# Late expert jobs of a fused retention, GLU and expert kernel: new order on the engine queues, the shared term kept in PSUM, unit 0 stores on ScalarE's queue

## The chip, the cores and the metric

The kernel runs on one core of a Trainium2 chip. The metric is the device time of one execution in microseconds (us). Five engines work side by side, each through a queue of its own in program order: PE (TensorE, matmuls into PSUM), DVE (VectorE), ACT (ScalarE), POOL (GpSimd) and SP (SyncE, which here only issues DMAs). Semaphores order them where one needs another's data or buffer.

## The reference

Retention over 4 x 8 heads of 576 positions gives 2304 tokens of 512 features; a gated unit follows; then the experts, where the late jobs of this case lie:

```python
P = np.exp(logits)                      # 2304 x 8, normalised 8 times over rows and columns
out = np.zeros((N, D), dtype=np.float32)
for e in range(E):                      # 8 experts
    h = np.maximum(x @ w1[e], 0.0)      # 2304 x 512 @ 512 x 1024
    ye = h @ w2[e]                      # 2304 x 1024 @ 1024 x 512
    out += P[:, e:e + 1] * ye
```

All is float32. The kernel reaches that precision by splitting every operand into a high and a low half and multiplying high x high, high x low and low x high.

## The kernel before

**Jobs.** The tokens form 3 units of 768, two halves of T = 384 each. A job is one unit, one expert and one of four groups of 256 hidden features: 96 jobs, numbered n. Jobs 0 to 31 are unit 0. Jobs 32 to 95, units 1 and 2, are the late jobs, and the change is about them. The weights that unit 0 prepared are kept in DRAM; a late job loads them again (`load_w1`, `load_w2`, 1792 KB each for w1 and w2).

**First products.** Both factors are cut in 2 x 2 blocks and multiplied with seven block products (Winograd's form) in place of eight. `block_product` (L767) is six matmuls of 384 columns into a PSUM bank px, py, pz or pv; its names are A11, S1, S2, A12, S3, S4, A22. Partial results move between banks by ACT copies (py <- px, pz <- py, p5 <- pv). DVE then masks (maximum with 0) and multiplies by the tokens' probabilities: the A12 product gives block A22 of the hidden matrix (L1090), S3 and S4 give z (L1102 to L1105), whose second half is block A11, and the A22 product gives block A12 (L1111).

**Operands of the second products.** They are A22, A11, A12 and four sums S1 to S4 of these, made by POOL (L1106, L1108, L1114, L1115). `part` makes the two halves of each: the high half is a cast on ACT (L970), the low half a subtraction (L971) on DVE, for S3 and S4 on POOL.

**Second products.** For each of two feature halves j there are seven steps of three matmuls (`second_product`, L977) in banks qx, qy, qz, qv: first (into qx, ACT copies it to qy), shared (qv), third (qy, copied to qz), c11 (qx), c22 (qz), c12 (qy), c21 (qz). Behind c11, c22, c12 and c21 a DVE addition (`gather`, L986) adds the bank to the output in SBUF. The shared term is added to `half_sums` in the same way, and at a unit's end to the four places that need it (L1031). In a unit's first job ACT copies take the place of the additions.

**Order.** The scheduler is off; the code's order is each queue's order. The loop at the end of the function writes job n's first products and, in the generators `second_products`, the second steps of job n - 1 between them; the last two pairs of steps run on into the next job. The stretch from job 32's start to job 33's is the opening: instead of second steps it has the last six output chunks of unit 0 (`outputs_of`, 512 columns), each added by DVE (L809) and stored (L811) by a DMA on SP's queue.

**Memory.** The blocks A22 and A12 (`h_blocks`), the sums and `half_sums` lie in `old`, the part of the output accumulator that unit 0 has left. Unit 0's last stores read from there.

**End of a unit.** `finish_unit` transposes the unit's output in six chunks (PE), copies each to a stage tile (ACT) and stores it (SP).

Of the kernel before, what the change touches and what calls it, by code (L numbers as in the profile page):

```python
# [9 lines left out]
F32 = mybir.dt.float32  # L10
# [3 lines left out]
ALU = mybir.AluOpType  # L14
# [9 lines left out]
E = 8  # L24
# [25 lines left out]
def retention_glu_experts(ctx: ExitStack, tc: tile.TileContext, a, out):  # L50
# [6 lines left out]
    nc = tc.nc  # L57
# [450 lines left out]
    sums = []  # L508
# [275 lines left out]
    def outputs_of(n):  # L784
# [3 lines left out]
        for t in range(NCH):  # L788
# [21 lines left out]
            if e == E - 1 and g == NPAIR - 1:  # L810
                nc.sync.dma_start(out[tt * 128:(tt + 1) * 128, :].rearrange("p (c d) -> p c d", c=2), o)  # L811
# [30 lines left out]
    for n, (u, e, g) in enumerate(jobs[:UJ]):  # L842
# [40 lines left out]
        if not n:  # L883
# [12 lines left out]
            w2_extra = ep.tile([128, 1536], F32R, name="w2_extra")  # L896
            next(weights)
# [43 lines left out]
    h_blocks, half_sums = old[:, 0], old[:, 2]  # L941
    sums = [old[:, k, h] for k in (1, 3) for h in range(2)]
# [8 lines left out]
    qx, qy, qz, qv = (pac.tile([128, 512], F32, tag="ac", name=n) for n in ("qx", "qy", "qz", "qv"))  # L951

# [13 lines left out]
    def part(n, i, engine=None):  # L966
        hi, lo = h_ops[n % 2][i]
        x = {A22: h_blocks[:, 0, :], A12: h_blocks[:, 1, :], A11: z[:, 1, :]}.get(i)
        x = sums[i - S1] if x is None else x
        nc.scalar.copy(hi, x)  # L970
        (engine or nc.vector).tensor_sub(lo, x, f32(hi))  # L971

    def second_product(n, j, x, w, ps, start=False):
        hi, lo = h_ops[n % 2][x]
        whi, wlo = (w2_pieces[n % 2][2 * (w + 7 * i) + j] for i in range(2))
        for i, (l, r) in enumerate(((whi, hi), (whi, lo), (wlo, hi))):
            nc.tensor.matmul(ps[:, :T], lhsT=l, rhs=r, start=start and i == 0, stop=i == 2, skip_group_check=True)  # L977

    def second_products(n):
        u, e, g = jobs[n]  # L980

        def gather(dst, ps):
            if (e, g) == (0, 0):
                nc.scalar.copy(dst, ps[:, :T])
            else:
                nc.vector.tensor_add(dst, dst, ps[:, :T])  # L986

        def at(k, h):
            return acc_d[:, k, u * UNIT + h * T:u * UNIT + (h + 1) * T]

        def first(j):
            second_product(n, j, A11, B11, qx, start=True)
            nc.scalar.copy(qy[:, :T], qx[:, :T])  # L993

        def shared(j):
            second_product(n, j, S1, T1, qv, start=True)
            gather(half_sums[:, j, :], qv)

        def third(j):
            second_product(n, j, S2, T2, qy)  # L1000
            nc.scalar.copy(qz[:, :T], qy[:, :T])

        def c11(j):
            second_product(n, j, A12, B21, qx)
            gather(at(j, 1), qx)

        def c22(j):
            second_product(n, j, S3, T3, qz)
            gather(at(2 + j, 0), qz)

        def c12(j):
            second_product(n, j, S4, B22, qy)
            gather(at(2 + j, 1), qy)

        def c21(j):
            second_product(n, j, A22, T4, qz)
            gather(at(j, 0), qz)

        for pair in (
            ((first, 0), (shared, 0)), ((third, 0), (c11, 0)), ((c22, 0), (c12, 0)), ((first, 1), (c21, 0)),  # L1020
            ((shared, 1), (third, 1)), ((c11, 1), (c22, 1)), ((c12, 1), (c21, 1)),
        ):
            for step, j in pair:
                step(j)
            yield

    def finish_unit(u, banks, stages):
        for j in range(2):
            for h in range(2):
                o = acc_d[:, 2 + j, u * UNIT + h * T:u * UNIT + (h + 1) * T]  # L1030
                nc.vector.tensor_add(o, o, half_sums[:, j, :])  # L1031
        yield
        for t in range(NCH):
# [6 lines left out]
            nc.scalar.copy(st, ps)  # L1040
# [3 lines left out]
    for p in (qy, qz):  # L1044
        nc.tensor.matmul(p, lhsT=sx[:, 0, 0, 0, :128], rhs=sx[:, 0, 0, :, :256], start=True, stop=True)
    load_probs(UJ)
    before, running, finishing = iter(()), iter(()), iter(())
    for n, (u, e, g) in list(enumerate(jobs))[UJ:]:
        first_job_of_late = n == UJ
# [5 lines left out]
        turn = u + 1 < NU and (e, g) == (E - 1, NPAIR - 1)  # L1055
        if g == NPAIR - 1:
            load_probs(n + 1)
        block_product(n, px, 0, "A11", start=True)
        nc.scalar.copy(py, px)
        if not first_job_of_late:  # L1060
            part(n - 1, S1)
        if (e, g) == (0, 0):
            next(switch)
        for _ in before:
            pass
        if n > UJ + 1:
# [12 lines left out]
        running = ys if first_job_of_late else second_products(n - 1)
        next(running)  # L1080
        block_product(n, py, 4, "S2")
        nc.scalar.copy(pz, py)
        if not first_job_of_late:
            part(n - 1, S3, nc.gpsimd)
            part(n - 1, S4, nc.gpsimd)
        if turn or (e, g) == (0, 0):
            next(switch)
        next(running)
        block_product(n, px, 1, "A12")
        nc.vector.scalar_tensor_tensor(h_blocks[:, 0, :], px, 0.0, pb[:, :T], ALU.max, ALU.mult)  # L1090
        part(n, A22)
        if turn:
            next(switch)
        next(running)
        next(finishing, None)
        block_product(n, pz, 5, "S3")
        if turn or ahead:
            next(switch)
        next(running)
        block_product(n, py, 2, "S4")  # L1100
        z = ev.tile([128, 2, T], F32, tag="z", name=f"z{n}")
        nc.vector.tensor_add(z[:, 1, :], pz, p5)  # L1102
# [3 lines left out]
        nc.gpsimd.tensor_add(sums[0], z[:, 0, :], h_blocks[:, 0, :])  # L1106
        part(n, A11)
        nc.gpsimd.tensor_sub(sums[1], sums[0], z[:, 1, :])  # L1108
        next(running)
        block_product(n, pz, 6, "A22")  # L1110
        nc.vector.scalar_tensor_tensor(h_blocks[:, 1, :], pz, 0.0, pb[:, T:], ALU.max, ALU.mult)  # L1111
        part(n, A12)
        next(running)
        nc.gpsimd.tensor_sub(sums[2], z[:, 1, :], z[:, 0, :])  # L1114
        nc.gpsimd.tensor_sub(sums[3], h_blocks[:, 1, :], sums[1])  # L1115
        next(finishing, None)
        if first_job_of_late:
            for _ in running:
                assert 0
        before = running  # L1120
    n = len(jobs)
    part(n - 1, S1)
    for _ in before:
        pass
    part(n - 1, S2)
    last = second_products(n - 1)
    next(last)
    part(n - 1, S3, nc.gpsimd)
    part(n - 1, S4, nc.gpsimd)
    for _ in last:  # L1130
        pass
    for _ in finish_unit(NU - 1, [qv, qx, px_all, qy, py_all, qz], [("xs", [128, 2, T]), ("z", [128, 2, T])]):
        pass
# [71 lines left out]
```

## Time and profile before

| | us |
|---|---|
| runs | 2245.19, 2249.09, 2249.39 (median 2249.09) |
| profiled execution | 2245.55, of which 2243.7 span |
| PE, DVE, ACT, POOL busy | 2096.1, 1477.2, 837.3, 817.5 |
| granted clock of TensorE, mean | 0.991 |

The span is from the first to the last instruction. Times in a timeline are counted from the span's start. Matmuls are pipelined and their busy times overlap, so the distance between the starts of two matmuls tells more than the length of one. A bracket at a row's end gives how long the engine stood idle ahead of it and whose work ended the wait.

### The profile page before, as it was taken

Reading aid. Unit: us, or ns where it says so; the run is one execution under the profiler, and the core shown is the slowest. Engines: PE = TensorE matmul, PEld = TensorE weight load, DVE = VectorE, ACT = ScalarE, POOL = GpSimd, SP = SyncE. Lnnn points to the kernel's source line nnn. Section 1 sums busy time; section 2 is a strip of 40 time slices with the busy share of each in tenths; the row PEclk is TensorE's granted clock in tenths of the full one; section 3 lists DMA queues with packets and bytes.
Section 4 is the critical chain, followed back from the end, with each engine's and each line's share of the span. In section 5 each row is a group of like instructions: output and inputs, shape, how many; then the busy total and the mean of one; then the engine's idle time right before and its main releaser. Section 6 shows DMA issues by size and latency. Waiting matters only on the chain.

```text
span 2243.7 us, 30431 instructions
## 1 busy us (share of the span) xinstructions
PE 2096.1 (93%) x11526; PEld 1877.4 (84%) x11526; DVE 1477.2 (66%) x2443; ACT 837.3 (37%) x1656; POOL 817.5 (36%) x748
## 2 busy tenths in 40 slices
PE   8999999999989999999979989989989999989987
PEld 5688789988878899999878888888878888888887
DVE  7854875543687777777746666666676666666665
ACT  4434322212444444444433333333344333333333
POOL 4312442200244545545333333343443433433342
PEclk9999999999999999999999999999999999999999
DMA  7410221100178888888766666566656665666562
GB/s 235 150 57 20 75 76 38 38 10 1 66 281 292 297 297 310 304 305 303 282 261 218 210 234 233 205 224 231 216 204 228 229 232 215 213 234 230 198 232 99
DMA packets 112690, 436.59 MB, mean 195 GB/s; under 512 B 12296, under 2 KB 30472, under 8 KB 96160
## 3 DMA queue, kind: packets, MB, share of 16 engines
q1 hardware_dynamic: 111680, 434.29, 54.3%
q8 instruction: 90, 1.47, 0.3%
q14 instruction: 56, 0.46, 0.1%
q10 hardware_dynamic: 864, 0.37, 0.1%
HBM read 312.40 MB, written 122.21 MB: 194 GB/s over the span
## 4 chain that ended last, share of the span: by engine, by line
PE 50%; issue 17%; POOL 15%; DVE 12%; ACT 2%; DMA 1%; POOLq 0%; DVEq 0%; SPq 0%; ACTq 0%
PE pz L767 5%; POOL xlo L971 5%; PE gv L173 4%; PE gv L174 4%; PE gv L175 4%; PE y L174 3%; PE y L175 3%; PE y L173 3%; POOL acc L1115 3%; PE py L767 3%; POOL acc L1108 3%; PE px L767 3%; DVE z L1105 3%; POOL acc L1106 3%; PE x L173 2%
## 5 line engine op out<-in xcount | busy, mean ns | idle before, releaser
L971 DVE TENSOR_TENSOR xlo<-acc,xhi 128x384 fp32r<-128x384 f32 x256 | 161.5, 631 | 162.8 <-ACT xhi L970 162.8
L970 ACT CAST xhi<-acc 128x384 fp32r<-128x384 f32 x384 | 190.2, 513 | 177.6 <-DVE acc L1111 98.5
L971 POOL TENSOR_TENSOR xlo<-acc,xhi 128x384 fp32r<-128x384 f32 x128 | 126.6, 1009 | 311.7 <-ACT xhi L970 311.7
L767 PE MATMUL py<-sx,w1s 128*128 128x384 f32 x1152 | 232.5, 336 | 0.0
L767 PEld LDWEIGHTS py<-sx,w1s 128*128 128x128 f32 x1152 | 204.1, 188 | 2.7
L1106 POOL TENSOR_TENSOR acc<-z,acc 128x384 f32<-128x384 f32 x64 | 65.0, 1016 | 383.5 <-DVE z L1105 383.5
L767 PE MATMUL px<-xhi,w1s 128*128 128x384 f32 x640 | 190.2, 337 | 0.0
L986 DVE TENSOR_TENSOR acc<-acc,qz 128x384 f32<-128x384 f32 x248 | 136.1, 549 | 62.5 <-PE qz L977 62.5
L576 POOL TENSOR_TENSOR t<-rw 128x256 f32<-128x256 f32 x32 | 47.0, 1469 | 240.1 <-issue 126.9
L174 PE MATMUL gv<-xlo,wslots 128*128 128x512 f32 (+2 forms) x368 | 126.6, 344 | 3.4 <-DVE xlo L407 2.1
L121 POOL TENSOR_SCALAR cv<-raw 128x512 f32<-128x512 f32 x36 | 63.2, 1759 | 181.5 <-DVE wslots L143 91.6
L173 PE MATMUL gv<-xhi,wslots 128*128 128x512 f32 (+2 forms) x368 | 127.7, 347 | 0.1
L175 PE MATMUL gv<-xhi,wslots 128*128 128x512 f32 (+2 forms) x368 | 126.2, 343 | 0.0
L809 DVE SCALAR_TENSOR_TENSOR acc<-y,prob,acc 128x512 f32<-128x512 f32 x168 | 118.0, 742 | 8.1 <-PE y L175 8.1
L767 PEld LDWEIGHTS px<-xhi,w1s 128*128 128x128 f32 x640 | 118.4, 188 | 0.4
L767 PE MATMUL pz<-sx,w1s 128*128 128x384 f32 x576 | 116.3, 336 | 0.0
L201 DVE TENSOR_TENSOR t<-t,gv 128x512 f32<-128x512 f32 (+2 forms) x66 | 38.8, 588 | 115.8 <-PE gv L175 115.8
L767 PE MATMUL pz<-xhi,w1s 128*128 128x384 f32 x384 | 114.3, 338 | 0.5 <-DVE z L908 0.5
L173 PE MATMUL y<-xlo,xhi 128*128 128x512 f32 x264 | 103.5, 392 | 10.3 <-DVE acc L809 10.3
L986 DVE TENSOR_TENSOR acc<-acc,qx 128x384 f32<-128x384 f32 x124 | 67.9, 548 | 66.4 <-PE qx L977 66.4
L993 ACT COPY qy<-qx 128x384 f32<-128x384 f32 x128 | 60.5, 473 | 129.3 <-PE qx L977 119.0
L767 PE MATMUL px<-xlo,w1s 128*128 128x384 f32 x320 | 107.6, 336 | 0.0
(315 smaller groups left out, 6067.3 us busy)
## 6 DMA issues: line engine op xcount, KB each, us to landing
w1s<-w_kept SPq DMA_DIRECT2D x64, 1792.0 KB, 7.2
w_kept<-w1s SPq DMA_DIRECT2D x32, 1792.0 KB, 6.6
rw<-in_w_dram SPq DMA_DIRECT2D x64, 512.0 KB, 5.6
w_kept<-xlo SPq DMA_DIRECT2D x64, 512.0 KB, 3.6
w2s<-w_kept SPq DMA_DIRECT2D x32, 1024.0 KB, 7.3
w_extra<-w_kept SPq DMA_DIRECT2D x32, 768.0 KB, 6.6
w_kept<-xlo SPq DMA_DIRECT2D x44, 384.0 KB, 4.2
w2c<-w_kept SPq DMA_DIRECT2D x32, 512.0 KB, 8.1
```

The costliest lines, as they stand in the source:

```text
L173: nc.tensor.matmul(ps, lhsT=lh, rhs=rh, start=start, stop=False)
L174: nc.tensor.matmul(ps, lhsT=lh, rhs=rl, start=False, stop=False)
L175: nc.tensor.matmul(ps, lhsT=ll, rhs=rh, start=False, stop=stop)
L767: nc.tensor.matmul(ps, lhsT=l, rhs=r[:, k, :], start=start and k == 0 and i == 0, stop=k == 1 and i == 2, skip_group_check=True,)
L809: nc.vector.scalar_tensor_tensor(o, y_2, pe, o, ALU.mult, ALU.add)
L970: nc.scalar.copy(hi, x)
L971: (engine or nc.vector).tensor_sub(lo, x, f32(hi))
L986: nc.vector.tensor_add(dst, dst, ps[:, :T])
L1105: nc.vector.scalar_tensor_tensor(z_2, z_2, 0.0, pb, ALU.max, ALU.mult)
L1106: nc.gpsimd.tensor_add(sums[0], z[:, 0, :], h_blocks[:, 0, :])
L1108: nc.gpsimd.tensor_sub(sums[1], sums[0], z[:, 1, :])
L1115: nc.gpsimd.tensor_sub(sums[3], h_blocks[:, 1, :], sums[1])
```

## The change

It rewrites the loop of the late jobs by hand. `part` is split into `high` (ACT) and `low` (DVE or POOL), and the generators are replaced by single steps, so that each queue gets its own order.

- The shared term stays in two PSUM banks, one per j, over a whole unit (`shared_sums`, pv and a new bank e1), and is added to the output once at the unit's end (`add_shared`). `half_sums` and its two additions per job go.
- pv is thereby taken, so the S1 product goes into qz, between the second steps that use qz.
- Block A22 has a tile of its own (`a22_block`); A12, S1 to S4 move within `old`.
- c12 and c21 of j = 1 of job n - 2 (called l) are the only steps that run over into job n; those of job n - 1 (called m) fill the rest. The high halves of A11, S1 and A12 are cast at the end of a job, that of S2 ahead of the copy py <- px.
- Unit 0's last six stores are issued by ACT. The two matmuls that set up qy and qz move from ahead of job 32 to its end.
- Behind the last job the steps of both j alternate over twice as many banks, and the copies of finished chunks alternate between ACT and DVE.

```diff
-                nc.sync.dma_start(out[tt * 128:(tt + 1) * 128, :].rearrange("p (c d) -> p c d", c=2), o)
+                nc.scalar.dma_start(out[tt * 128:(tt + 1) * 128, :].rearrange("p (c d) -> p c d", c=2), o)
...
+            a22_block = ep.tile([128, T], F32, name="a22_block")
...
-    h_blocks, half_sums = old[:, 0], old[:, 2]
-    sums = [old[:, k, h] for k in (1, 3) for h in range(2)]
+    h_blocks = [a22_block, old[:, 0, 0]]
+    sums = [old[:, k, h] for k, h in ((1, 0), (0, 1), (1, 1), (2, 0))]
...
+    def shared(n, j):
+        second(n, j, S1, T1, shared_sums[j], start=jobs[n][1:] == (0, 0))
...
         block_product(n, px, 0, "A11", start=True)
+        if not opening:
+            high(m, S2)
         nc.scalar.copy(py, px)
+        if not opening:
+            high(m, S3)
+            low(m, S1)
+            low(m, A12)
...
+        if l >= UJ:
+            c12(l, 1)
+            c21(l, 1)
+            add_12(l, 1)
+            add_21(l, 1)
...
+            low(m, S2)
+            block_product(n, py, 4, "S2")
+            nc.scalar.copy(pz, py)
...
+            first(m, 0)
+            high(m, S4)
+            low(m, S3, nc.gpsimd)
+            low(m, S4, nc.gpsimd)
+            shared(m, 0)
+            block_product(n, qz, 3, "S1", start=True)
+            nc.scalar.copy(p5, qz)
...
+            third(m, 0)
+            c11(m, 0)
+            add_11(m, 0)
         block_product(n, px, 1, "A12")
...
+            c22(m, 0)
+            add_22(m, 0)
+            c12(m, 0)
+            add_12(m, 0)
+        high(n, A22)
+        low(n, A22)
         block_product(n, pz, 5, "S3")
...
+            first(m, 1)
+            c21(m, 0)
+            add_21(m, 0)
         block_product(n, py, 2, "S4")
...
+            third(m, 1)
+            shared(m, 1)
+        nc.gpsimd.tensor_add(sums[0], z[:, 0, :], h_blocks[0])
+        high(n, A11)
         nc.gpsimd.tensor_sub(sums[1], sums[0], z[:, 1, :])
         block_product(n, pz, 6, "A22")
...
+            c22(m, 1)
+            add_22(m, 1)
+        low(n, A11)
+        if not opening:
+            c11(m, 1)
+            add_11(m, 1)
         nc.gpsimd.tensor_sub(sums[2], z[:, 1, :], z[:, 0, :])
+        nc.gpsimd.tensor_sub(sums[3], h_blocks[1], sums[1])
+        high(n, S1, A12)
```

How the queues stand, at three places. In the rows an operation's output stands left of the arrow; `acc` is the output accumulator, which also holds the sums, and `xhi` and `xlo` hold the high and low halves.

**DVE, from the mask of the A22 product to the subtraction of S2, where a job meets the next.** Before (the subtractions are the lows of A12, S1 and S2):

```order
L1111 SCALAR_TENSOR_TENSOR acc<-pz,prob_b_9543 128x384
L971 TENSOR_TENSOR xlo<-acc,xhi 128x384
L986 TENSOR_TENSOR acc<-acc,qx 128x384
L986 TENSOR_TENSOR acc<-acc,qz 128x384
L971 TENSOR_TENSOR xlo<-acc,xhi 128x384
L986 TENSOR_TENSOR acc<-acc,qy 128x384
L986 TENSOR_TENSOR acc<-acc,qz 128x384
L971 TENSOR_TENSOR xlo<-acc,xhi 128x384
```

Now (the lows of A11, then of S1 and A12 as one row with x2, then of S2):

```order
L1157 SCALAR_TENSOR_TENSOR acc<-pz,prob_b_9544 128x384
L989 TENSOR_TENSOR acc<-acc,qz 128x384
L975 TENSOR_TENSOR xlo<-z_11570,xhi 128x384
L989 TENSOR_TENSOR acc<-acc,qx 128x384
L975 TENSOR_TENSOR xlo<-acc,xhi 128x384 x2
L989 TENSOR_TENSOR acc<-acc,qy 128x384
L989 TENSOR_TENSOR acc<-acc,qz 128x384
L975 TENSOR_TENSOR xlo<-acc,xhi 128x384
```

Before, the low of A11 stands ahead of the mask, and the additions that free qx and qz stand between the lows. Now three lows stand ahead of the additions of c12 (qy) and c21 (qz).

**PE, from the A11 product of a job, as far as the bank qz is used again.** Before (c12, c21, then S1 into pv):

```order
L767 MATMUL px<-x_more,w1s_5290 128x384 x6
L977 MATMUL qy<-xhi,w_extra 128x384
L977 MATMUL qy<-xlo,w_extra 128x384
L977 MATMUL qy<-xhi,w2c_9545 128x384
L977 MATMUL qz<-xhi,w_extra 128x384
L977 MATMUL qz<-xlo,w_extra 128x384
L977 MATMUL qz<-xhi,xlo 128x384
L767 MATMUL pv<-x_more,w1s_5290 128x384 x6
```

Now (c21 of the job before last, S2, first, shared, then S1 into qz):

```order
L981 MATMUL qz<-xhi,xlo 128x384
L767 MATMUL py<-sx,w1s_5290 128x384 x6
L981 MATMUL qx<-xhi,w2s_5291 128x384
L981 MATMUL qx<-xlo,w2s_5291 128x384
L981 MATMUL qx<-xhi,w2c_9546 128x384
L981 MATMUL pv<-xhi,w2s_5291 128x384
L981 MATMUL pv<-xlo,w2s_5291 128x384
L981 MATMUL pv<-xhi,w2s_5291 128x384
L767 MATMUL qz<-x_more,w1s_5290 128x384 x6
```

Before, c21 uses qz one step after c12, and c22 had filled qz two steps earlier. Now S2, first and shared stand between c21 and the next use of qz, which is S1.

**ACT in the opening, job 32, now:**

```order
L1091 COPY p_32_9561<-pv 128x384
L811 DMA out_dram<-acc 256x1x256
L1094 COPY pz<-py 128x384
L612 CAST xhi<-acc 128x2x384
L811 DMA out_dram<-acc 256x1x256 x2
L971 CAST xhi<-a_block 128x384
L811 DMA out_dram<-acc 256x1x256 x2
L971 CAST xhi<-z_9620 128x384
L811 DMA out_dram<-acc 256x1x256
```

The six stores stood on SP, behind the loads of job 33's w1 and job 32's w2. They now stand on ACT, between the copies and casts of the opening.

## Rows read from the trace of the kernel before

**Rows 1.** The page, section 1: busy us (share of the span) xinstructions of each engine.

```profile
PE 2096.1 (93%) x11526; PEld 1877.4 (84%) x11526; DVE 1477.2 (66%) x2443; ACT 837.3 (37%) x1656; POOL 817.5 (36%) x748
```

**Rows 2.** Windows: stretch, length, busy of each engine, granted clock, DMA share, GB/s.

```profile
952.00:1008.00 56.00, 56.00 (x282) 50.62 (x281) 41.83 (x55) 23.75 (x36) 28.46 (x31) 1.00 0.86 309
1392.49:1409.56 17.07, 15.49 (x86) 14.45 (x86) 11.15 (x20) 6.16 (x15) 6.46 (x7) 1.00 0.61 217
```

**Rows 3.** Timeline of PE, job 49: start us, us, engine, line, operation [idle before].

```profile
1403.91 1.20 PE L767 MATMUL py<-sx,w1s 128*128 128x384 f32 x6
1404.95 0.33 PE L977 MATMUL qv<-xhi,w_extra 128*128 128x384 f32 x1
...
1408.30 1.23 PE L767 MATMUL px<-x_more,w1s 128*128 128x384 f32 x6
...
1409.72 0.34 PE L977 MATMUL qy<-xhi,w2c 128*128 128x384 f32 x1
1411.46 0.45 PE L977 MATMUL qz<-xhi,w_extra 128*128 128x384 f32 x1 [1.40 <-DVE acc L986]
...
1425.36 1.20 PE L767 MATMUL px<-x_more,w1s 128*128 128x384 f32 x6
```

**Rows 4.** Waits of PE, late stage: us in total, times, longest.

```profile
PE qz L977 <- DVE acc L986: 89.1, 65, 2.4
```

**Rows 5.** Timeline of DVE, ACT and POOL, end of job 48 and start of 49.

```profile
1405.14 0.56 DVE L1103 TENSOR_TENSOR z<-py,p 128x384 f32<-128x384 f32 x1
...
1406.73 0.51 ACT L970 CAST xhi<-z 128x384 fp32r<-128x384 f32 x1 [2.68 <-DVE z L1105]
1406.78 1.02 POOL L1106 TENSOR_TENSOR acc<-z,acc 128x384 f32<-128x384 f32 x1 [5.46 <-DVE z L1105]
...
1407.28 0.93 DVE L971 TENSOR_TENSOR xlo<-z,xhi 128x384 fp32r<-128x384 f32 x1 [0.58 <-ACT xhi L970]
...
1407.87 1.22 POOL L1108 TENSOR_TENSOR acc<-acc,z 128x384 f32<-128x384 f32 x1
...
1409.06 1.00 POOL L1114 TENSOR_TENSOR acc<-z 128x384 f32<-128x384 f32 x1
...
1409.72 0.75 DVE L971 TENSOR_TENSOR xlo<-acc,xhi 128x384 fp32r<-128x384 f32 x1 [0.58 <-ACT xhi L970]
...
1410.03 1.31 POOL L1115 TENSOR_TENSOR acc<-acc 128x384 f32<-128x384 f32 x1
...
1410.87 0.54 DVE L986 TENSOR_TENSOR acc<-acc,qz 128x384 f32<-128x384 f32 x1
```

**Rows 6.** Timeline of DVE and POOL in a unit 0 job and in job 62.

```profile
1074.10 0.95 DVE L613 TENSOR_TENSOR x_more<-acc,x_more 128x768 fp32r<-128x768 f32 x1
...
1074.26 1.39 POOL L576 TENSOR_TENSOR t<-rw 128x256 f32<-128x256 f32 x1 [2.61 <-DVE w1s L587]
...
1074.97 1.76 DVE L741 TENSOR_TENSOR w2s<-rw,w2s 128x1024 fp32r<-128x1024 f32 x1
...
1633.98 2.22 DVE L971 TENSOR_TENSOR xlo<-acc,xhi 128x384 fp32r<-128x384 f32 x1
```

**Rows 7.** Opening of the late stage: timelines of PE, SP, DVE; DMA issues (us to landing).

```profile
1111.01 1.20 PE L767 MATMUL px<-x_more,w1s 128*128 128x384 f32 x6
...
1139.37 1.23 PE L767 MATMUL px<-x_more,w1s 128*128 128x384 f32 x6
...
1114.52 0.95 SPq L964 DMA_DIRECT2D prob_b<-prob_kept  x1
...
prob_b<-prob_kept SPq DMA_DIRECT2D x1, 384.0 KB, 6.1
...
1130.90 0.56 DVE L1090 SCALAR_TENSOR_TENSOR acc<-px,prob_b 128x384 f32<-128x384 f32 x1 [12.32 <-DMA out_dram<-acc]
```

**Rows 8.** Tail: timelines of PE and ACT.

```profile
2217.41 0.35 PE L977 MATMUL qy<-xhi,w2s 128*128 128x384 f32 x1
...
2233.79 0.59 ACT L1040 COPY st<-qv 128x512 f32<-128x512 f32 x1 [4.70 <-PE qv L1038]
```

More of the change, by code (lines that the diff above doesn't have):

```diff
@@ L950, in retention_glu_experts @@
     h_ops = [[halves(p, i) for i in range(7)] for p in range(2)]
-    qx, qy, qz, qv = (pac.tile([128, 512], F32, tag="ac", name=n) for n in ("qx", "qy", "qz", "qv"))
     def load_w2(n):
@@ L964, in load_probs, with operand, high, low @@
             nc.sync.dma_start(prob_b[e % 2], prob_kept[e, (u - 1) * UNIT:u * UNIT].partition_broadcast(128))
[L966 to L970, printed above, removed]
+    def operand(n, i):
+        return h_ops[n % 2][i], {A22: h_blocks[0], A12: h_blocks[1], A11: z[:, 1, :]}.get(i, sums[(i - S1) % 4])
+    def high(n, *parts):
+        for i in parts:
+            (hi, _), x = operand(n, i)
+            nc.scalar.copy(hi, x)
+    def low(n, i, engine=None):
+        (hi, lo), x = operand(n, i)
         (engine or nc.vector).tensor_sub(lo, x, f32(hi))
-    def second_product(n, j, x, w, ps, start=False):
+    def second(n, j, x, w, ps, start=False):
         hi, lo = h_ops[n % 2][x]
@@ L976, in second_product, with gather @@
         for i, (l, r) in enumerate(((whi, hi), (whi, lo), (wlo, hi))):
-            nc.tensor.matmul(ps[:, :T], lhsT=l, rhs=r, start=start and i == 0, stop=i == 2, skip_group_check=True)
-    def second_products(n):
+            nc.tensor.matmul(ps, lhsT=l, rhs=r, start=start and i == 0, stop=i == 2, skip_group_check=True)
+    def gather(n, k, h, ps):
         u, e, g = jobs[n]
[L982 to L1025, printed above, removed]
@@ L1027, in finish_unit, with banks_of, first @@
-    def finish_unit(u, banks, stages):
+        dst = acc_d[:, k, u * UNIT + h * T:u * UNIT + (h + 1) * T]
+        if (e, g) == (0, 0):
+            nc.scalar.copy(dst, ps)
+        else:
+            nc.vector.tensor_add(dst, dst, ps)
+    def banks_of(n, j):
+        if n == len(jobs) - 1 and j:
+            return px, py, pz, shared_sums[j]
+        return qx, qy, qz, shared_sums[j]
+    def first(n, j):
+        x, y, z, e = banks_of(n, j)
+        second(n, j, A11, B11, x, start=True)
+        nc.scalar.copy(y, x)
@@ new lines, in shared, with third, c11, c22 @@
+    def shared(n, j):
+        second(n, j, S1, T1, shared_sums[j], start=jobs[n][1:] == (0, 0))
+    def third(n, j):
+        x, y, z, e = banks_of(n, j)
+        second(n, j, S2, T2, y)
+        nc.scalar.copy(z, y)
+    def c11(n, j):
+        second(n, j, A12, B21, banks_of(n, j)[0])
+    def c22(n, j):
+        second(n, j, S3, T3, banks_of(n, j)[2])
+    def c12(n, j):
+        second(n, j, S4, B22, banks_of(n, j)[1])
+    def c21(n, j):
+        second(n, j, A22, T4, banks_of(n, j)[2])
@@ L1112, in retention_glu_experts @@
-        part(n, A12)
-        next(running)
-        nc.gpsimd.tensor_sub(sums[2], z[:, 1, :], z[:, 0, :])
[L1115 to L1128, printed above, removed]
@@ new lines, in retention_glu_experts @@
+        low(n, A11)
+        if not opening:
+            c11(m, 1)
+            add_11(m, 1)
+        nc.gpsimd.tensor_sub(sums[2], z[:, 1, :], z[:, 0, :])
+        nc.gpsimd.tensor_sub(sums[3], h_blocks[1], sums[1])
+        high(n, S1, A12)
+    n, l = len(jobs) - 1, len(jobs) - 2
+    high(n, S2, S3)
+    low(n, S1)
+    low(n, A12)
+    c12(l, 1)
+    add_12(l, 1)
+    first(n, 1)
+    c21(l, 1)
+    add_21(l, 1)
+    low(n, S2)
+    first(n, 0)
+    high(n, S4)
+    low(n, S3, nc.gpsimd)
@@ L1133, in retention_glu_experts @@
+    low(n, S4)
+    for step in (shared, third, c11):
+        for j in (1, 0):
+            step(n, j)
+            if step is c11:
+                add_11(n, j)
+    add_shared(NU - 1)
+    for step, add in ((c22, add_22), (c12, add_12), (c21, add_21)):
+        for j in (1, 0):
+            step(n, j)
+            add(n, j)
+    for _ in finish_unit(NU - 1, [shared_all, qx_all, px_all, py_all], [("xs", [128, 2, T]), ("z", [128, 2, T])]):
         pass
```

105 lines of the change are left out of this document (58 added, 47 removed).

## The prediction

> **What bounds the kernel now.** I went from the page to the windows, the waits of PE, and then one late job engine by engine. On the page PE is busy for 93% of the span [rows 1], which says little: the windows give 56.00 of 56.00 us in the stage with the unit 0 jobs but 15.49 of 17.07 us in a late job, at a granted clock of 1.00 in both [rows 2]. So the late jobs lose PE time, and not to the clock. Their length is 1425.36 - 1408.30 = 17.06 us [rows 3]. Six matmuls of 384 columns take 1404.95 - 1403.91 = 1.04 us, 0.1733 us each, and a job has 84 of them (7 block products of 6, 14 second steps of 3): 14.56 us. The other **2.50 us a job** is waiting. The waits name one place: qz behind a DVE addition, 89.1 us over the late stage [rows 4]; in the timeline the next matmul was due 0.17 us after 1409.72 and started at 1411.46, 1.57 us late [rows 3]. DVE shows why: the addition that frees qz ran at 1410.87 to 1411.41, behind the low halves of A11 and A12, and one of these started at 1407.28 and took 0.93 us, the other 0.75 us [rows 5]. The same operation takes 0.55 us elsewhere, so something held it. The remaining 0.9 us is smaller waits of this kind.
>
> The holder is POOL. The low that started at 1407.28 ended at 1408.21, 0.41 us after POOL's operation of 1406.78 ended; the one of 1409.72 ended at 1410.47, again 0.41 us after a POOL end (1410.06) [rows 5]. The other way round, POOL's operation of 1410.03 ended at 1411.34, 0.87 us after that low, instead of after 1.00 us [rows 5]. The two engines take turns on subtractions and additions that read SBUF twice; DVE operations with a PSUM input (0.54 us at 1410.87, beside POOL) aren't held. When both wait, they alternate: POOL's operation of 1074.26 got in when one DVE operation ended (1075.05), and the next DVE operation, queued right behind, took 1.76 us because it waited for POOL's end at 1075.65 [rows 6].
>
> **The change, part by part.** Times t count from the start of the A11 product of a job, with PE never waiting.
>
> *Shared sum in PSUM.* Two DVE additions per job go (0.54 us each); four at the end of a unit stay. DVE isn't full (idle a third of the span [rows 1]), so this counts only where PE waits for DVE, in the next part.
>
> *Queues reordered.* I laid the new order on the old durations. On PE, c12 and c21 of the job before last now stand at t = 1.04 to 2.08, before S2; S1 goes to qz at t = 4.16; S4's product ends at t = 11.44, A22's at 13.52, c22 at 14.04. A DVE operation starts 0.19 us after the matmuls it needs (1404.95 to 1405.14), POOL's first sum 1.64 us after that start (1406.78), and its four sums start 1.09, 1.19 and 0.97 us apart [rows 5]. That puts the first sum at 13.27 to 14.28, the second at 14.36 to 15.36. DVE: the masked A22 product 13.72, the c22 addition 14.24, then the low of A11 at 14.70. It meets the second sum and ends at 15.36 + 0.41 = 15.77. The third sum was waiting: 15.77 + 0.87 = 16.64. The c11 addition (0.54, unheld) ends at 16.24; the low of S1, at 16.15, waits and ends at 17.05; the fourth sum ends at 17.92; the low of A12, at 16.97, ends at 18.33. Then the additions of c12 and c21, to 19.26, and PE may start S1 into qz at 19.31, which is t = 4.75 of the next job. It is due at 4.16: **0.59 us of waiting**, and 0.11 for the restart (the first matmul after a wait takes 0.45 us, others 0.34 [rows 3]).
>
> Where else could PE wait? S2 needs the copy py <- px, which stands on ACT behind the high half of S2: second sum at 15.36, cast to 15.9 (0.51 us [rows 5]), copy to t = 1.8, due 2.08: hidden by 0.25 us. c21 needs the c22 addition: done at t = 0.23, due 1.56. The third steps' low of S2 is done at t = 5.05, due 5.9. The lows of S3 and S4 on POOL end at 4.7 and 6.3, due 7.9 and 8.4. Other steps have over 0.5 us. I add 0.05 us for bubbles between blocks. A job: 14.56 + 0.59 + 0.11 + 0.05 = **15.3 us**, against 17.06.
>
> The queue of loads: SP's load of w1 still waits for A22's product, its load of w2 for c21, now at t = 2.1 instead of 3.8. A job loads two times 1792 KB, 3.67 MB; at 15.3 us that is 240 GB/s, where the row of unit 0 moved 309 [rows 2]. Taken as hidden; the price if not is a rival below.
>
> *Opening of the late stage.* DVE's masked product waits 12.32 us for the store of unit 0's rows, whose place it overwrites [rows 7]. In the change it writes a tile of its own and needs only the probabilities, issued at 1114.52 and landed 6.1 us later, at 1120.6 [rows 7]. The DVE work behind it up to the last output addition (five additions and masks of 0.55 us, the mask of 0.96, four output additions of 0.7, and 1 us in which ACT issues stores and makes the high half) ends near 1128.1; the two matmuls that set up qy and qz now wait for that, so the next job starts at 1128.7 instead of 1139.37: 10.7 us. Bounds: 15.5 us of matmuls from 1111.01 (42 of 0.173 and 36 of 512 columns, so 0.23 each) give 1126.5; stores that are as late as before, by a 12.32 us wait behind the load burst, hold POOL's sums back about 5 us, so 1134. The ACT queue also waits for each of six output additions before it issues a store; behind it are copies that PE needs one product later, and I count at most 1 us of it in the 1128.7.
>
> The row shows a store waiting behind a burst of loads. The Trainium skill (Trainium Kernel Development and Optimization, Key Constraints) says that transfers issued from different queues run on the same 16 engines and interleave, so that another queue saves issue time only. By that rule the stores land no sooner than before, and the end of the opening is the later bound, 1134; the sum would be about 2130. No row here shows two queues with loads at once.
>
> *The 63 further jobs.* Before: 1139.37 to 2217.41 [rows 7, 8], 1078.0 us. After: the first has 78 matmuls and no job before last, 13.7 us; 62 of 15.3 are 948.6; two jobs whose additions are on ACT don't wait (-1.3). The unit change in the middle costs some 7 us now (1078.0 - 63 x 17.06 = 3.3, and the short first two jobs hide 4); I keep 7 and add 3, an estimate, because the transposes there ran in gaps that close. Sum 971.0, so 107.0 less.
>
> *Tail.* From 2217.41 to the first copy of finished rows 16.4 us pass [rows 8]. In the new order the same DVE queue ends its last addition at 12.5 (low of S2 at 5.05, shared additions to 9.6, six more of 0.48), and four transposes and a copy start at 13.5: 2.9 less. The stores behind it stay, each copy waits for the store two before.
>
> **Sum:** 10.7 + 107.0 + 2.9 = 120.6 less than the profiled execution's 2245.55 us, **2125 us**. The median of the runs shown, 2249.09, is 0.16% above that execution; about 0.2% is what can be told from no change.
>
> **Rivals.** *A, no turn is lost:* DVE keeps its place when two lows follow each other. The low of A12 then ends at 17.46, qz is free at t = 3.9, and a job takes 14.6: 62 x 0.7 = 43 less, **2082**. Against it is the alternation in [rows 6]; for it, that this is one instance at another spot. The Trainium skill (SBUF — State Buffer, "Who interferes with whom") states that a VectorE instruction with two SBUF inputs and a GpSimd one that reads SBUF exclude each other, in order of issue; POOL's fourth sum issues before the low of A12, so by that rule A doesn't come. The trace agrees [rows 5, 6]. Chance 0.2.
>
> *B, one turn more:* POOL gets two operations in before the low of A12 (the fourth sum, then the low of S3). 0.87 more a job, 54 in all: **2179**. The high half of S3 is ready in time for it (t = 2.6). Against it, the alternation. Chance 0.13.
>
> *C, the loads bound it:* if the queue gave no more than the 217 GB/s of the late row [rows 2], 3.67 MB would take 17 us, jobs stay as long as now, and only the two ends remain: **2232**. Against it is the 309 beside it. Chance 0.03.
>
> *D, slower:* the lows wait for POOL as long as the longest one did, 2.22 us at 1633.98 [rows 6], beside a POOL operation of twice the width. Three such lows in a row are 6.6 us in place of 3.3, so qz is late by 4.0 us, a job takes 18.6, and 62 of them cost 95 us while the ends give 14: **2327**. It turns slower once the three lows lose 1.7 us more than reckoned. POOL's sums take 1.0 to 1.31 us in every row of a late job, so chance 0.02.
>
> **How the numbers follow.** Forecast 0.62, with its own range 2105 to 2145 (the opening's bounds, 3 us for the unit change, 0.2 us a job). The 80% range takes in A and part of B: 2078 to 2165. Faster by over 0.2%: all but part of C and D, 0.97; same 0.01; slower 0.02.
>
> **What would show it.** Job starts 15.3 us apart; in PE's waits, a block product into qz behind a DVE addition, 0.5 to 0.7 us in each of some 60 jobs, and hardly another; the three lows of A11, S1, A12 at about 1.07, 0.90 and 1.36 us, POOL's last two sums at 1.3; first late job 17 to 18 us long, DVE waiting there for the probabilities. Jobs of 14.6 with lows of 0.55 would mean A; of 16.2 B; waits for a DMA in the job C. A wait of PE for ACT before S2 would mean that the slack of 0.25 us was wrong.

## The result, and the profile after

| | us |
|---|---|
| before, 4 runs | 2245.19 to 2249.39, median 2247.48 |
| after, 4 runs | 2131.57 to 2136.81, median 2131.98 |
| after / before | 0.9491, 95% interval 0.9474 to 0.9509 |
| forecast | 2125, range 2078 to 2165 |

The change takes 115.5 us off the median; the time is 7 us above the forecast. The profiled execution is the slowest of the four (2136.81 us, 2134.9 of it span): its first 56 us were granted 0.82 of the clock (0.94 in the profile of before), and job 32 starts 4.1 us later in it (1115.14 against 1111.01). So distances are compared below, not times since the span's start.

The page of after, busy time of each engine (compare [rows 1]):

```profile
PE 2058.7 (96%) x11526; PEld 1884.9 (88%) x11526; DVE 1480.1 (69%) x2323; ACT 860.3 (40%) x1649; POOL 846.5 (40%) x747
```

PE is now busy for 96% of a shorter span. Its waits from the start of the late jobs on, after (what waited, for whom; total, times, longest; compare [rows 4]):

```profile
PE qz L767 <- DVE acc L989: 29.3, 59, 2.0
PE py L767 <- ACT py L1072: 5.8, 2, 5.3
PE pv L981 <- DVE acc L1037: 1.9, 1, 1.9
PE py L981 <- DVE xlo L975: 1.1, 1, 1.1
PE pz L767 <- DVE z L1133: 1.0, 1, 1.0
```

The 89.1 us for qz have become 29.3 in 59 waits, 0.5 us in each, now ahead of a block product (L767). No DMA stands in the list. The second line is new, and is the part that the forecast missed.

One late job in PE's timeline, after (compare [rows 3]):

```profile
1397.68 1.20 PE L767 MATMUL px<-x_more,w1s 128*128 128x384 f32 x6
...
1401.66 0.34 PE L981 MATMUL pv<-xhi 128*128 128x384 f32 x1
1402.48 1.34 PE L767 MATMUL qz<-x_more,w1s 128*128 128x384 f32 x6 [0.48 <-DVE acc L989]
...
1413.02 1.20 PE L767 MATMUL px<-x_more,w1s 128*128 128x384 f32 x6
```

From one A11 product to the next 15.34 us pass, where it was 17.06. By starts, the S1 product was due 0.17 us after 1401.66 and came 0.65 us late; the 0.48 in the bracket is the idle time alone. DVE ahead of that wait, after (compare [rows 5]):

```profile
1397.38 0.54 DVE L989 TENSOR_TENSOR acc<-acc,qz 128x384 f32<-128x384 f32 x1
1397.84 1.07 DVE L975 TENSOR_TENSOR xlo<-z,xhi 128x384 fp32r<-128x384 f32 x1
1398.84 0.54 DVE L989 TENSOR_TENSOR acc<-acc,qx 128x384 f32<-128x384 f32 x1
1399.30 2.19 DVE L975 TENSOR_TENSOR xlo<-acc,xhi 128x384 fp32r<-128x384 f32 x2
1401.42 0.54 DVE L989 TENSOR_TENSOR acc<-acc,qy 128x384 f32<-128x384 f32 x1
1401.89 0.54 DVE L989 TENSOR_TENSOR acc<-acc,qz 128x384 f32<-128x384 f32 x1
```

And POOL beside it:

```profile
1397.48 1.02 POOL L1154 TENSOR_TENSOR acc<-acc,z 128x384 f32<-128x384 f32 x1
1398.45 1.34 POOL L1173 TENSOR_TENSOR acc<-z 128x384 f32<-128x384 f32 x1
1399.76 1.33 POOL L1174 TENSOR_TENSOR acc<-acc 128x384 f32<-128x384 f32 x1
1401.05 1.32 POOL L975 TENSOR_TENSOR xlo<-acc,xhi 128x384 fp32r<-128x384 f32 x1
```

The low of A11 takes 1.07 us and ends 0.41 us after POOL's operation of 1397.48; the lows of S1 and A12 take 2.19 together; the additions, with one operand in PSUM, keep their 0.54 beside the same POOL operations. POOL's operations, 1.0 us when alone, take 1.32 to 1.34. The addition that frees qz ends at 1402.43, and the product starts 0.05 us later.

The first two late jobs on PE, after: the A11 products of jobs 32, 33 and 34, and the S2 product of job 33 (compare [rows 7]).

```profile
1115.14 1.20 PE L767 MATMUL px<-x_more,w1s 128*128 128x384 f32 x6
...
1132.40 1.20 PE L767 MATMUL px<-x_more,w1s 128*128 128x384 f32 x6
1138.93 2.29 PE L767 MATMUL py<-sx,w1s 128*128 128x384 f32 x6 [5.32 <-ACT py L1072]
...
1153.00 1.20 PE L767 MATMUL px<-x_more,w1s 128*128 128x384 f32 x6
```

The opening is 17.26 us, where it was 28.36. Job 33 is 20.60, where it was 14.85 (1139.37 to 1154.22): half of the gain is given back at once. ACT shows what stood ahead of the copy that the S2 product waits for (ACTq is ACT issuing a DMA):

```profile
1135.42 0.54 ACTq L811 DMA_DIRECT2D out_dram<-acc  x1
1136.00 0.92 ACT L971 CAST xhi<-acc 128x384 fp32r<-128x384 f32 x2 [2.73 <-DVE xlo L975]
1137.99 0.51 ACT L971 CAST xhi<-acc 128x384 fp32r<-128x384 f32 x1 [1.06 <-POOL acc L1154]
1138.41 0.47 ACT L1072 COPY py<-px 128x384 f32<-128x384 f32 x1
```

The copy's input was complete at about 1133.5. Ahead of it in ACT's queue were a store, which waited for the last output addition, and the high halves of S1, A12 and S2. The addition and the sums waited for DVE and POOL, and these for unit 0's stores to leave `old`:

```profile
1134.17 0.56 DVE L1157 SCALAR_TENSOR_TENSOR acc<-pz,prob_b 128x384 f32<-128x384 f32 x1 [2.03 <-DMA out_dram<-acc]
1134.65 0.74 DVE L809 SCALAR_TENSOR_TENSOR acc<-y,prob,acc 128x512 f32<-128x512 f32 x1
```

```profile
1134.20 1.00 POOL L1152 TENSOR_TENSOR acc<-z,a_block 128x384 f32<-128x384 f32 x1 [27.58 <-DMA out_dram<-acc]
1136.62 1.33 POOL L1154 TENSOR_TENSOR acc<-acc,z 128x384 f32<-128x384 f32 x1 [1.42 <-DMA out_dram<-acc]
```

The granted clock, last but two in the row, fell behind the 5.3 us wait (a window of after; 1.00 is 2.4 GHz, and 0.50 would be 1.2 GHz):

```profile
1137.50:1142.00 4.50, 3.07 (x10) 3.07 (x11) 1.98 (x2) 1.86 (x4) 3.97 (x4) 0.63 0.97 402
```

From 1138.93 the next twelve matmuls take 3.66 us, where 12 of 0.173 are 2.08: 1.6 us more.

The two matmuls that set up qy and qz, at the end of the opening:

```profile
1132.05 0.33 PE L1165 MATMUL qy<-sx 128*128 128x384 f32 x1
```

They ran 2.6 us ahead of the last output addition (1134.65, above).

The end: the c12 step that opens the tail, and the first copy of finished rows (compare [rows 8]):

```profile
2111.48 0.33 PE L981 MATMUL qy<-xhi,w2s 128*128 128x384 f32 x1
```

```profile
2124.90 0.58 ACT L1050 COPY st<-pv 128x512 f32<-128x512 f32 x1 [6.52 <-PE pv L1045]
```

13.4 us lie between them, 16.4 before.

### The profile page after: what moved, and what is told of

The parts are those of the page before. It is cut to its first block, busy times and chain, and to the rows that moved or that the text cites. A ratio compares the mean times of both kernels' runs of the same rounds, so it can differ in the third digit from the quotient of the medians.

```text
span 2134.9 us, 30383 instructions
## 1 busy us (share of the span) xinstructions
PE 2058.7 (96%) x11526; PEld 1884.9 (88%) x11526; DVE 1480.1 (69%) x2323; ACT 860.3 (40%) x1649; POOL 846.5 (40%) x747
## 4 chain that ended last, share of the span: by engine, by line
PE 71%; DVE 20%; ACT 1%; DMA 1%; issue 1%; POOL 0%; DVEq 0%; SPq 0%; POOLq 0%; ACTq 0%
PE pz L767 9%; DVE xlo L975 9%; PE py L767 6%; PE px L767 6%; DVE acc L989 6%; PE qy L981 5%; PE gv L173 4%; PE gv L175 4%; PE gv L174 4%; PE qz L767 4%; PE y L174 4%; PE y L175 4%; PE y L173 4%; PE qx L981 3%; PE qz L981 3%; PE x L173 2%
## 5 line engine op out<-in xcount | busy, mean ns | idle before, releaser
L1152 POOL TENSOR_TENSOR acc<-z,a_block 128x384 f32<-128x384 f32 x64 | 64.9, 1015 | 509.2 <-DVE z L1146 481.7
L767 PE MATMUL py<-sx,w1s 128*128 128x384 f32 x1152 | 233.0, 337 | 6.0 <-ACT py L1072 5.8
L767 PEld LDWEIGHTS py<-sx,w1s 128*128 128x128 f32 x1152 | 203.7, 188 | 10.0 <-ACT py L1072 7.3
L767 PE MATMUL px<-xhi,w1s 128*128 128x384 f32 x640 | 188.9, 335 | 0.0
L971 ACT CAST xhi<-acc 128x384 fp32r<-128x384 f32 x320 | 158.1, 514 | 74.6 <-POOL acc L1152 35.4
L975 DVE TENSOR_TENSOR xlo<-acc,xhi 128x384 fp32r<-128x384 f32 x193 | 178.1, 949 | 2.7 <-ACT xhi L971 2.6
L975 POOL TENSOR_TENSOR xlo<-acc,xhi 128x384 fp32r<-128x384 f32 x127 | 148.9, 1172 | 43.6 <-ACT xhi L971 43.6
L767 PEld LDWEIGHTS px<-xhi,w1s 128*128 128x128 f32 x640 | 118.3, 188 | 0.4
L767 PE MATMUL pz<-sx,w1s 128*128 128x384 f32 x576 | 115.6, 335 | 0.0
L767 PE MATMUL pz<-xhi,w1s 128*128 128x384 f32 x384 | 113.8, 336 | 1.5 <-DVE z L1133 1.0
L767 PE MATMUL px<-xlo,w1s 128*128 128x384 f32 x320 | 107.1, 335 | 0.0
```

The lines of the kernel that those rows point to most:

```text
L767: nc.tensor.matmul(ps, lhsT=l, rhs=r[:, k, :], start=start and k == 0 and i == 0, stop=k == 1 and i == 2, skip_group_check=True,)
L1152: nc.gpsimd.tensor_add(sums[0], z[:, 0, :], h_blocks[0])
```

## The experiments

Two questions: what holds the 0.5 us a job and the wait of job 33, and which part of the change made the opening short. The theory for the first is the turn-taking of [rows 5, 6]; the rivals are the amount of work on DVE or POOL, and the loads.

**One low moved behind the additions** that free qy and qz.

```diff
             low(m, S1)
-            low(m, A12)
...
             add_21(l, 1)
...
+        if not opening:
+            low(m, A12)
```

> The change with the low half of A12 moved on DVE behind the additions that free qy and qz; no work is added or taken away. Theory (three lows stand between the A22 mask and these additions, each losing a turn to a POOL sum, and only that holds S1's product): qz is free at t = 3.4 instead of 4.75, due 4.16, the wait of 0.5 us a job goes, jobs take 14.6 to 14.7 us instead of 15.3, and the time falls by 60 x 0.7 = 42 us to about 2090. Rival (the wait is the bank's: S1 put into qz comes too soon behind c21, whatever DVE's order): jobs stay at 15.3, time 2132.

Measured: 2092.48 us, ratio to before 0.9313 (0.9298 to 0.9329). DVE in a late job:

```profile
1386.36 0.90 DVE L975 TENSOR_TENSOR xlo<-acc,xhi 128x384 fp32r<-128x384 f32 x1
1387.18 0.54 DVE L989 TENSOR_TENSOR acc<-acc,qy 128x384 f32<-128x384 f32 x1
1387.65 0.54 DVE L989 TENSOR_TENSOR acc<-acc,qz 128x384 f32<-128x384 f32 x1
1388.11 1.88 DVE L975 TENSOR_TENSOR xlo<-acc,xhi 128x384 fp32r<-128x384 f32 x2
```

The lows of A12 and S2 still lose their turns (1.88 us for two), but behind the addition, where PE doesn't wait. Nearly every job is 14.6 us (14.56 to 14.64), against 14.56 of matmuls: nothing is left to win there. Loads don't bind at this length either (255 GB/s between 1300 and 1400, and no wait of PE for a DMA).

**One low more ahead of the additions**, the opposite edit.

```diff
             low(m, A12)
+            low(m, S2)
...
         else:
-            low(m, S2)
             block_product(n, py, 4, "S2")
```

> One more low ahead of the addition that frees qz: low(m, S2) stands behind low(m, A12) on VectorE, ahead of the two additions of the job before the last, and not behind them. Nothing is added or taken away. Theory (the first product into qz waits for the addition of c21, and each low ahead of it costs a turn at the SBUF ports next to a GpSimd sum): the addition into qz comes 0.9 to 1.0 us later in each of 63 jobs, the wait qz <- DVE acc grows from 29.3 to about 85 to 95 us, the job from 15.3 to 16.2 to 16.3, and the time is 2188 to 2198 us. Rival (the 15.3 us is VectorE's or GpSimd's amount of work per job, or the granted clock, and not what stands ahead of that one addition): the same instructions in another order, 2127 to 2140 us.

Measured: 2237.17 us in one run, above both expectations. The direction is the theory's, the size is not. The waits of PE for qz, DVE, and PE in one job:

```profile
PE qz L767 <- DVE acc L989: 104.0, 59, 2.3
```

```profile
1406.72 3.47 DVE L975 TENSOR_TENSOR xlo<-acc,xhi 128x384 fp32r<-128x384 f32 x3
1410.12 0.54 DVE L989 TENSOR_TENSOR acc<-acc,qy 128x384 f32<-128x384 f32 x1
1410.59 0.54 DVE L989 TENSOR_TENSOR acc<-acc,qz 128x384 f32<-128x384 f32 x1
```

```profile
1411.18 1.87 PE L767 MATMUL qz<-x_more,w1s 128*128 128x384 f32 x6 [1.76 <-DVE acc L989]
1412.85 0.52 PE L981 MATMUL qy<-xhi,w2s 128*128 128x384 f32 x1
1413.17 0.52 PE L981 MATMUL qy<-xlo,w2s 128*128 128x384 f32 x1
```

Three lows take 3.47 us for 2.19 of two: the third adds 1.28 us, its own time included, which is the distance at which POOL's operations follow each other beside the lows (1.29 to 1.31 in after), and not 0.9 to 1.0. The job becomes 16.6 us. And in 16 of the 63 jobs it is 18.2, where the granted clock fell behind the wait of 1.76 us: the matmuls from 1412.85 on start 0.32 us apart instead of 0.17. Two stretches of 84 matmuls, one behind each of two such waits (granted clock again last but two; the second stops short of the wait that follows it):

```profile
1394.70:1411.10 16.40, 14.72 (x84) 14.40 (x84) 12.01 (x18) 6.40 (x14) 6.91 (x6) 1.00 0.58 221
1411.10:1427.90 16.80, 16.41 (x84) 16.09 (x84) 10.68 (x17) 6.24 (x14) 6.85 (x6) 0.90 0.51 194
```

The waits for qz are 74.7 us longer than in after (104.0 for 29.3) and 16 falls of 1.6 are 26, together 100; the profiled execution's span is 100.4 us longer (2235.3 for 2134.9). Why the clock fell in these 16 jobs and not in the others, with the same wait, stays open.

**The shared sum back in SBUF**, with its two additions per job on DVE:

```diff
-        second(n, j, S1, T1, shared_sums[j], start=jobs[n][1:] == (0, 0))
+        second(n, j, S1, T1, shared_sums[j], start=True)
+        if jobs[n][1:] == (0, 0):
+            nc.scalar.copy(old[:, 3, j], shared_sums[j])
+        else:
+            nc.vector.tensor_add(old[:, 3, j], old[:, 3, j], shared_sums[j])
...
-                nc.vector.tensor_add(o, o, shared_sums[j])
+                nc.vector.tensor_add(o, o, old[:, 3, j])
```

> The change with one part undone: the shared term is started anew in its bank in every job and added to a sum in SBUF by DVE, two additions of 0.54 us more per job, behind the low of S2 and behind the mask of z. Theory (DVE counts only between the A22 mask and the c21 addition): both additions lie in gaps, jobs stay at 15.3, time within 5 us of 2132. Rival (DVE's amount of work sets the job): 2 x 0.47 us in 63 jobs, about 59 us more, near 2190.

Measured: 2135.14 us in one run; jobs of 15.33, the wait for qz 30.6 us in 60 waits for 29.3 in 59. The additions find room. With the rest of the change in place, keeping the sum in PSUM is worth nothing that a run can tell; the gain of the jobs comes from the rest, the order on the queues. What each single step of that order is worth, the change of bank for S1 among them, wasn't measured apart.

**The sums S3 and S4 on DVE** behind the additions, in place of POOL; the high half of S3 moves with them:

```diff
-            high(m, S3)
...
+        if not opening:
+            nc.vector.tensor_sub(sums[2], z[:, 1, :], z[:, 0, :])
+            nc.vector.tensor_sub(sums[3], h_blocks[1], sums[1])
+            high(m, S3)
...
-        nc.gpsimd.tensor_sub(sums[2], z[:, 1, :], z[:, 0, :])
-        nc.gpsimd.tensor_sub(sums[3], h_blocks[1], sums[1])
...
```

> The change with the sums S3 and S4 made by DVE instead of POOL, behind the additions that free qy and qz: DVE has 1.1 us more work per job, but nothing of POOL's beside the lows of S1 and A12. Theory (turns with POOL): these two lows take 0.55 us instead of 2.19 us together, qz is free at t = 3.6, jobs take 14.6 to 14.9 us (the cast of S3 then stands ahead of two copies on ACT, up to 0.25 us of wait), time 2090 to 2108. Rival (DVE's amount of work sets the job): jobs of 15.3 or longer, up to 16.4.

Measured: 2112.51 us in one run, 4.5 above the range of the theory; jobs of 14.93 to 14.95. DVE has more to do, and the lows of S1 and A12 together take 1.01 us, not 2.19:

```profile
1392.11 1.01 DVE L975 TENSOR_TENSOR xlo<-acc,xhi 128x384 fp32r<-128x384 f32 x2
```

So POOL's presence beside them cost the time, not the work on DVE. The jobs stay 0.3 us above those of the first experiment; the weight loads of PE (PEld) name the reason, from 1300 to 1500:

```profile
PEld qy L981 <- ACT qy L999: 5.3, 13, 0.4
```

The high half of S3 now comes later on ACT and ahead of a copy that PE needs: the wait moved to another queue, 0.4 us in each of 13 jobs.

**The stores back on SP.**

```diff
-                nc.scalar.dma_start(out[tt * 128:(tt + 1) * 128, :].rearrange("p (c d) -> p c d", c=2), o)
+                nc.sync.dma_start(out[tt * 128:(tt + 1) * 128, :].rearrange("p (c d) -> p c d", c=2), o)
```

> The change with the six stores of unit 0 back on SP's queue. Theory (the stores land late because they share the DMA engines with the load burst, whoever issues them): the late stage's opening, 21.7 us from the start of job 32 to that of 33 in the changed kernel, and the 5.3 us wait in job 33 change together by less than 4 us; jobs stay at 15.3. Rival (a queue of its own is what brings the stores forward): they land some 5 us later and the two grow by 5 us or more.

Measured: 2132.59 us in one run, which can't be told from after. From the product of job 32 to that of job 34 it takes 39.57 us (16.30 + 23.27), against 37.86 (17.26 + 20.60) in after, 1.7 us more. The mask of the A22 product waits longer for the stores, and the S2 product behind it too:

```profile
1133.05 0.56 DVE L1157 SCALAR_TENSOR_TENSOR acc<-pz,prob_b 128x384 f32<-128x384 f32 x1 [5.13 <-DMA out_dram<-acc]
```

```profile
1136.13 1.33 PE L767 MATMUL py<-sx,w1s 128*128 128x384 f32 x3 [6.75 <-ACT py L1072]
```

A store lands 8.5 us after its issue here (median) and 8.3 in after: the queue makes them no faster. The mask runs 21.2 us after the start of job 32 here and 19.0 in after. But one profile is thin evidence for 1.7 us: the four other experiments on the change that leave the opening alone take 37.8 to 39.2 us from job 32 to job 34, so by these profiles ACT's queue is worth between 0.3 and 1.8 us here.

**The two parts alone, on the kernel before.** The tile:

```diff
+            a22_block = ep.tile([128, T], F32, name="a22_block")
...
-    h_blocks, half_sums = old[:, 0], old[:, 2]
+    h_blocks, half_sums = [a22_block, old[:, 0, 1]], old[:, 2]
```

> The kernel before with one part of the change alone: the A22 block of the hidden values gets a tile of its own and is no more written over unit 0's outputs. Theory (in the opening, VectorE stands 12.3 us at the A22 mask for the stores, and the output additions and the job's other work are queued behind it): the mask runs when the probabilities have landed, about 1120 to 1122, the wait for the stores moves to the A12 mask and the GpSimd sums, and the opening is 22 to 23 us for 28.4: 2240 to 2244 us, before being 2249. Rival (the opening is bound by the landing of the stores whichever instruction waits for it): opening 27 to 29 us, 2247 to 2250.

The queue, as in the first lines of the change's diff:

> The kernel before with the other part alone: the stores of unit 0 are issued by ScalarE, not by SyncE. The A22 mask still waits for the stores of the block it writes over. Theory (the stores share the DMA engines with the loads whichever queue issues them, and the issue behind the loads is worth about 2 us): the opening is 25 to 28 us for 28.4, the mask on VectorE still stands 8 to 12 us for the stores, 2246 to 2249 us. Rival (the stores were late because they stood behind the loads in SyncE's queue): landing within 3 us of issue, the mask waits under 4 us, the opening is 20 us or less, 2240 us or less.

Measured: 2243.67 us with the tile, 2256.27 with the queue, one run each, and 2243.9 to 2248.07 (median 2246.38) for the kernel before on that chip. These two profiles reach job 32 at 1115.29 and 1117.49, 4.3 and 6.5 us later than that of before, in code that neither edit touches, so the distances on PE say more than the times:

| | opening | job 33 | sum |
|---|---|---|---|
| before | 28.36 | 14.85 | 43.21 |
| tile alone | 16.21 | 21.75 | 37.96 |
| queue alone | 25.94 | 23.42 | 49.36 |
| after | 17.26 | 20.60 | 37.86 |

The tile alone does what the change does here (5.25 of 5.35 us); its opening came out shorter than expected, and job 33 gave 6.9 of the 12.2 back. DVE with the tile, where the one long wait of [rows 7] has become one for the probabilities and one for the stores:

```profile
1125.15 0.56 DVE L1091 SCALAR_TENSOR_TENSOR a_block<-px,prob_b 128x384 f32<-128x384 f32 x1 [2.26 <-DMA prob_b<-prob_kept]
...
1136.26 0.56 DVE L1112 SCALAR_TENSOR_TENSOR acc<-pz,prob_b 128x384 f32<-128x384 f32 x1 [4.36 <-DMA out_dram<-acc]
```

The queue alone costs 6 us in these two jobs (its run is 9.9 us above the median), which neither side expected. DVE's mask still stands 10.01 us (the stores land 9.2 us after issue, median; the profile puts this wait down to a load that landed last); the additions behind it are late, ACT waits for each before it issues its store, and all of ACT's work waits with it:

```profile
1145.00 0.55 ACTq L811 DMA_DIRECT2D out_dram<-acc  x1
1145.59 0.46 ACT L1059 COPY py<-px 128x384 f32<-128x384 f32 x1 [1.87 <-DVE acc L809]
```

The last store is issued at 1145.00; ACT's copy into `half_sums`, whose place that store reads, runs at 1152.60, and PE waits 5.4 us for the copy qz <- qy behind it. That the copy waited for this store is inferred: the profile names no releaser for it.

**The opening in another order**, on top of the first experiment: the last two output chunks ahead of the A22 product, the copy of job 33 ahead of three high halves.

```diff
-        if not opening:
+        if m > UJ:
             high(m, S2)
         nc.scalar.copy(py, px)
+        if m == UJ:
+            high(m, S1, A12, S2)
...
+        if opening:
+            for _ in ys:
+                pass
         block_product(n, pz, 6, "A22")
...
-        high(n, S1, A12)
+        if not opening:
+            high(n, S1, A12)
```

> The version with low(m, A12) behind the additions, and the opening in another order: the last two output chunks of unit 0 ahead of the A22 product, and the copy py <- px of job 33 ahead of the high halves of S1, A12 and S2 on ScalarE. Theory (the second wait of job 33 is the copy standing behind high halves whose sums waited for the stores of unit 0): the copy runs at once behind its product, the 5.4 us wait py <- ACT py and the matmuls at half clock behind it go, a wait of at most 1.5 us for the S1 operands comes in their place, and the time falls by 3 to 6 us, 2086.5 to 2089.5. Rival (the stores themselves hold job 33, through the GpSimd sums that are written where they read from, so the wait only moves to the S1 products): 2091 to 2093 us, as without the edit.

Measured: 2089.11 us, ratio to before 0.9298 (0.9282 to 0.9313), the fastest version here, inside the theory's range. The opening is 15.99 us, job 33 18.41, together 34.40 for 39.24 (17.24 + 22.00) in the first experiment: 4.8 less. By the runs alone the two can't be told apart (0.9313 and 0.9298, intervals that overlap); the distances tell them apart, since no version of the change with the old opening order took less than 37.8. Two of PE's waits in job 33:

```profile
1134.01 1.31 PE L767 MATMUL py<-sx,w1s 128*128 128x384 f32 x6 [1.69 <-ACT py L1072]
...
1136.58 0.46 PE L981 MATMUL qx<-xhi,w2c 128*128 128x384 f32 x1 [0.41 <-DMA w2c<-w_kept]
```

The first is 1.69 us for 5.4. Two more follow, 0.22 for a low half and 1.44 for a copy on ACT behind a high half, so 3.8 us of waiting stay, and POOL's sums still start when the stores have landed. What else the edit brings back is the clock: 1.00 over the whole of job 33, for 0.84 in the first experiment. So the copy's place in ACT's queue cost a part of job 33, and the stores hold the rest; how much of the gain belongs to the earlier output chunks, the other half of the edit, isn't separated.

## Why the prediction was right, and where it was off

*What bounds the kernel, and the job.* Confirmed. The job was put at 15.3 us and is 15.29 to 15.34; the S1 product was to be 0.59 us late and is 0.65; the three lows were put at 1.07, 0.90 and 1.36, they take 1.07 and 2.19 for the last two together; POOL's last two sums at 1.3, they take 1.34 and 1.33. The alternation read from [rows 5, 6] carried the number, and the two opposite edits show that it is the cause: one low fewer ahead of the addition ends the wait, one more makes it 1.76 us, and without POOL's sums beside them two lows take 1.01 us. The Trainium skill (SBUF — State Buffer, "Who interferes with whom") states that a VectorE instruction with two SBUF inputs and a GpSimd one that reads SBUF exclude each other, in order of issue. The trace agrees: lows of 0.55 us take 0.90 to 1.3 beside POOL, and additions with a PSUM operand keep 0.54.

*Slack of the copies.* Confirmed in the steady jobs, wrong in job 33. The step "S2 needs the copy py <- px, which stands on ACT behind the high half of S2 [...] hidden by 0.25 us" was worked out for a job whose sums wait for nothing. The sign that the prediction had named for this, a wait of PE for ACT before S2, is there: 5.32 us.

*Opening.* Forecast 17.7 us, measured 17.26, and that is in part luck. The prediction had job 33 wait for the last output addition, through the two matmuls that set up qy and qz. They didn't wait for it: they ran 2.6 us ahead of it. DVE waited for the probabilities as forecast (1.9 us), but the last addition came 3.2 us later than reckoned, behind a mask that waited 2.03 us more for the stores. PE had one wait of 1.0 us in the opening, for z; 16.0 of the 17.26 us are matmuls.

*The 63 further jobs.* This is the term that failed: 971.0 forecast, 2111.48 - 1132.40 = 979.1 measured, and 6.9 of the 8.1 lie in its first job, "78 matmuls and no job before last, 13.7 us", which took 20.60. The prediction had the cause in hand, as a bound on the opening ("stores that are as late as before [...] hold POOL's sums back about 5 us, so 1134"), but set it at the end of the opening and didn't take it. There PE isn't held. The sums and the last store hold the high halves, these hold the copy in ACT's queue, and that holds the S2 product of the next job, with 1.6 us more at the lower clock. The Trainium skill (Trainium Kernel Development and Optimization, Key Constraints) has transfers of different queues share the 16 engines; by it the sum was put at about 2130. The trace agrees on the transfers: the stores landed in 8.3 us from ACT's queue, 8.5 from SP's. It doesn't on the place: the opening did not get longer, job 33 did. So it is luck in part that 2130 lies so near 2131.98.

*Unit change and tail.* Job 63 to job 70, around the unit change, take 9.2 us more than eight jobs of 15.32, and 10 were kept. Two of them, 64 and 65, ran at a granted clock of 0.91. In the run with the stores on SP it was 1.00 there, and the same eight jobs take 6.1 us more. So the 10 us were some 4 too many, and the clock hid it in the profiled execution. The tail was put at 13.5 us and is 13.4, with DVE's last addition ending at 12.7 where 12.5 was reckoned; no experiment took its parts apart.

*Rivals.* A did not come: the lows lost their turns. Its price was right, since the first experiment makes jobs of 14.6 us by other means. B did not come, nor C: no PE wait names a DMA, at 15.3 or at 14.6 us a job, but for 0.41 us in job 33 of the fastest version. D did not come: the longest low of a late job takes 1.39 us, not 2.22. But its turning point, 1.7 us a job more, left out the clock: with one low more ahead of the addition the wait grew by 1.3 us, and with 16 falls of the clock the time, 2237, was only 9 us under before.

The terms as measured: 28.36 - 17.26 = 11.1, 1078.0 - 979.1 = 98.9, 16.4 - 13.4 = 3.0, together 113.0 for 120.6 forecast. The two profiled executions differ by 108.7, and the later one loses 4.1 of it before job 32.

## What to carry to other kernels

When two engines take turns at a shared resource, count the turns ahead of the one instruction that another engine waits for, and move only those: the low of A12 was free behind the addition, and cost 0.7 us a job ahead of it. When a wait is taken from one instruction, follow the data to the next that needs the late transfer, and then along every queue behind that one: here the wait went from DVE's mask through POOL's sums to a copy on ACT, into the next job. A store issued from a compute engine's queue makes all of that engine's work wait for the store's input: with the tile's order it paid by less than 2 us in the profiles, without it it cost 6.

## What the runs showed that was not expected

- When several subtractions stand in a row next to POOL, each further one adds 1.28 us, not the 0.9 to 1.0 read from single ones.
- A PE wait of 1.76 us per job let the granted clock fall in 16 of 63 jobs (0.90 over the stretch behind such a wait), while the waits of 1.40 to 1.43 us in the jobs of before left the matmuls at 0.17 us apart.
- Moving the six stores to ACT alone made the first two late jobs of the kernel before 6 us slower.
- Two more additions per job on DVE, already busy for 69% of the span, cost nothing that a run can tell (2135.14 against 2131.57 to 2136.81).
